# A gated mix of memory attention and a ReGLU layer: later places for the gate's row products, and a new written-out order of work

## The chip, the cores and the metric

The kernel runs on one core of one Trainium2 chip. The metric is device time in microseconds (us), the median of several runs; less is better. Before the change it was 268.71 us, the median of three runs of 266.35, 268.71 and 269.01 us.

## What is computed

`x` is 2048 rows of 512 numbers in bfloat16. The result is `g * a + (1 - g) * b` with a gate for each row, `g = sigmoid((x * gate_w).sum(-1))`.

```
a (attention with memory): q, k, v = x @ wq, x @ wk, x @ wv, 32 heads of 16; 4 segments s of 512 rows
    a_dot = softmax(q_s k_s^T / 4 + causal mask) v_s
    a_mem = phi(q_s) M / (phi(q_s) z);   phi(t) = t + 1 if t > 0, else exp(t)
    o = sigmoid(beta) * a_mem + (1 - sigmoid(beta)) * a_dot
    M, z = M + phi(k_s)^T v_s, z + sum phi(k_s)       (used by the next segment)
    a = o @ wo
b (ReGLU layer): b = (relu(x @ W_gate) * (x @ W_up)) @ W_down,   512 -> 1792 -> 512
```

The sum inside the gate, `(x * gate_w).sum(-1)`, is what is called the gate's row product here: one VectorE instruction for 128 rows.

## The kernel before, in words

**Work and stages.** The four segments are pipelined. `proj(s)` (L528) makes q, k and v of a segment, `att(s)` (L633) its attention, `mu(s)` (L581) the memory products phi(k)^T v that are added to `M`, `nd(s)` (L602) the part read from the memory, `ffn(s)` (L729) the 14 column blocks of `W_gate` and `W_up`, and `outp(s)` (L753) the four output tiles with `wo` and `W_down`. While the attention of one segment runs, the projections of the next, the ffn of this one and the outputs of the last one are put between its pieces on TensorE.

**PSUM.** There are eight banks. Four (`psL`) hold the logits of one attention quad; the next quad has to wait until ScalarE has made the exponentials of the last (`exp`, L651). The other four (`psA`) are handed out in turn to everything else: one bank for each accumulation, as one *epoch*. A bank may be written anew when all readers of the epoch before it are done. The list `BANKS` says which bank each new epoch gets. So a matmul can be held up by a VectorE or ScalarE instruction that has still to empty a bank.

**The names used below.** `wg0_8` and `wu0_8` are the products of column block 8 of `W_gate` and `W_up` for segment 0 (L739), two halves of two matmuls each. `relu0_8` (L747 on ScalarE, L748 on VectorE) empties the bank of the first into `rl`; `hm0_8` (L750, VectorE) multiplies the bank of the second with it into `hT` and so frees that bank. `q2_1`, `k2_1` and `v1_2` are projections (L544, L546), emptied by `qcp2_1`, `kcp2_1`, `vcp1_2` (VectorE at L555, L559, L572, ScalarE at L551). `quad0_2C` is one attention quad (L647), `pv0_1` a product of exponentials and values (L679), emptied by two transposes `tr0_1_0`, `tr0_1_1` (L689); after it come `rden`, `rdg`, `ad` and `bt` (L696 to L705) on VectorE. `kmask` (L563, L564) makes the masked k, and `kts`, `kphi`, `qts`, `qphi` (L525, L526) the phi of k and q.

**The gate (L481 to L513).** The rows of segment 0 are in `hT` already. For the twelve row tiles 4 to 15 the SP queue loads 128 rows into one shared buffer, `osb` slot 2 (`ldxr4` to `ldxr15`, L494), and VectorE makes the product `gate4` to `gate15` (L497) from it, in place. With one buffer, `ldxr5` waits for `gate4`. The four sums of a segment go through `gexp` and `omg1` on ScalarE, and by way of a scratch tensor in DRAM (`gwr`, `grd`, L504 and L506) they are spread for `rdg`.

**What sets the order.** Nothing is scheduled on the chip. Every operation is put into a queue of one engine (L390 to L513, L820 to L851). `ORDER` (L24) is a text with a letter for each operation: the letter names the queue, and the next operation of that queue that is not done is placed. Operations that two engines can do (`relu`, `qcp`, `kcp`, `vcp`, `kmask`, `fin`) stand in queues of both, so the letter also picks the engine. `place` (L204) puts the operation at the end of its engine's program, with the semaphore waits that it needs. Every engine then does its program strictly in this order. The times in the code (a cost for each operation, `LAT`, and `op.after`, the earliest time of an operation) are what the order was planned with; in `place`, `after` is read for DMAs alone (L230), and the costs decide nothing there but which of 16 DMA semaphores a transfer gets (L232). The order itself stands in the text.

**The loads of the gate** have planned earliest times (L495): `GATE_T` is 44000 ns for tiles 4 to 7, 90000 for 8 to 11 and 140000 for 12 to 15, and 4000 ns more for each further tile.

Of the kernel before, what the change touches and what calls it, by code (L numbers as in the profile page):

```python
# [21 lines left out]

LETTERS = "abcdefghijklmnopqrstuvwxyzABCDEFGHIJKLMNOPQRSTUVWXYZ0123456789"
ORDER = (  # L24
    "gefafafefafefafefaefaggfgagggggahgihaisggsagggsgsahgsigssahsisssasbsssassssassssCassssBsasssCsasBabsasEsasHaEHsasyIaDpasaIwsIasDasaFsaysSIapsaFSwauIau"
    "FasLubSsIapjFSuwSukaunuLSuKSapkuwnuVuLSuSVnuKpdunwuLSudSuLSuSmRpdmuKkSswLSudlnuSLuSsokKRsCuSRUpswRuUDSssSLsUCSsIpJDSqUSwQsIozSsuCIpzSsxSszdSswDSssQdsB"
    "uESudIpJLsSSwsdRsFSuuLsxScpzqFSwuPszqcLToTyzpSsTzwuScuFSsTLsSszySpcSsFSwuBSsszcRuuELSUpSuzwunUuzsuLSKouSIpJuLSwuSzsSsLSssBSEsSQpCuQwsuRsRqDUySpSLuSwUz"
    "uSuzunuKuzSopLKSuSwIuuzIuzssKLSpSCszSuwSnuuLsSouEQqLSySpzVswsVzsFsuzGSpnuwuzLSsSuzuKszSpmSGouSwrLtSSOtOuOmStnpWStSwItIortSOtOtOSuSNpWSLtwSsXstFSqSpztw"
    "szsztBtSpztwzortSOztStSMSpOXStwOStStIWtIrntxtOSoOtSOxpSuSMWswtQXuRsRqESpnUtwuPSuLUTuTLuTtAopqLSTQuwzSuStzSuLuSpzsSLwSuntuzoQsKpBSuwStzuuILSuJSuLSptSzw"
    "sSnstDSsNSpAswXRuBSuSuLumSuLmoSpnqSLwSRuszUsSzuSEuUQKuzSpzsLSowuIuIuzsKSzuSuCLSuSrAKuuOOuLpuwOuuLqLSpSzVuwsVzuzuLuSpzsLwSuSDsSuzuKsSzsSGAsuSWGpSLswrsO"  # L30
    "tOFtSOpStwIWrItSOtOSotOtSWpStwStSMrXtOuxOSuOSpKtnWwtQuouQqLxSpSztSwuSzuQttLSptSnwtIotItzSNuzzpXuwSzuSuLStSLtSpnqwsAosPStTFtSqSTSpSzuwTtzSuTMuuzXStnKpz"
    "mtSzmowtuLSuSuzuSLuSKpSnuAwotIrLSttOItOSpOSuwSuSuLtuMSpuSLwXurLuuOuOSLpSuwSOuSuLuuLSqKSSpSzuwuzuLuuzKSpzuwzuuLSSuLuSpSzqSwLuAVzuVuSKzpSuwSzuzLSuuzuKpS"
    "zuSwLuSuSAuuLWSuLSpKuSWwSutLtuSpSuwSuLStttStSupLtwrtOtOMtSOXtSuSWtSrtOpOtOwuWtLttMSSqXSSpztwtztztzuzutSzuSuAtSKtSuNptXwutuLSpuSLwuLutqLSSpSzuwSuzuLuuz"
    "SuLSuKzpzuwuSzuSuAtKSuLSpuSLwSuuLuuSuStKSpLtSwutqSpSztwuzuMuuLKXSpuSzwSuzuLSvzvKpSzuwSuAuLSvSuSuKSuSvLuSuqKvzvzuvzuzvzvLvvzvvAvvvNvXNvvXvvvvvvNvvvXvvv"
    "vvvvNvvvvvXMX"
)
BANKS = (
    "012312301230123012301231021302130120123102132031201320321031203102130123012302300123121202312102102101201031203123012010231023120302030201201203203203"
    "10202012010231023102310213021302023001321310230230230320302021032132132130"
)  # L40


# [275 lines left out]
def program(sc, nc, T, PL, PA, A_x, A_wq, A_wk, A_wv, A_wo, A_beta, W_g, W_u, W_d, gate_w, out, NSEG, KT, NF, NT, EPS, SCALE):  # L318
    V = type("V", (), T)

    def op(eng, fn, occ, **k):
        return sc.add(Op([(eng, fn, occ)], **k))

    def pe(fn, occ, **k):
        k.setdefault("lat", PE_LAT)
        if k.get("role") == "w":
            k["reads"] = list(k.get("reads", ())) + [f"init{i}" for i in range(4)]
        return op("pe", fn, occ, **k)

    def dve(fn, occ, **k):  # L330
        return op("dve", fn, occ, **k)
# [151 lines left out]
    gq = {"pe": [], "act": [], "dve": [], "pool": [], "sp": []}  # L483
    for c in range(NSEG):
        t0, t1 = 4 * c, 4 * c + 4
        gx = V.gexp[:, t0:t1]
        if c == 0:
            for t in range(4):
                gq["dve"].append(dve(lambda e, t=t: e.tensor_tensor_reduce(out=V.hT[:, t, :], in0=V.hT[:, t, :], in1=V.gwb[:], scale=1.0, scalar=0.0, op0=ALU.mult, op1=ALU.add, accum_out=V.gl[:, t:t + 1]),
                                     690, reads=[f"hT{t}", "gwb"], writes=[f"hT{t}", f"gl{t}"], name=f"gate{t}"))  # L490
                gq["dve"][-1].after = 5800.0
        else:
            for t in range(t0, t1):
                ld = dma("sp", lambda e, t=t: e.dma_start(V.osb[:, 2, :], A_x[0, t * 128:(t + 1) * 128, :]), 1 << 17, writes=["osb2_0", "osb2_1"], name=f"ldxr{t}")  # L494
                ld.after = GATE_T[c] + 4000.0 * (t - t0)  # L495
                gq["sp"].append(ld)
                gq["dve"].append(dve(lambda e, t=t: e.tensor_tensor_reduce(out=V.osb[:, 2, :], in0=V.osb[:, 2, :], in1=V.gwb[:], scale=1.0, scalar=0.0, op0=ALU.mult, op1=ALU.add, accum_out=V.gl[:, t:t + 1]),  # L497
                                     690, reads=["osb2_0", "osb2_1", "gwb"], writes=["osb2_0", "osb2_1", f"gl{t}"], name=f"gate{t}"))
# [79 lines left out]
    def va(s):  # L578
        return [f"va{s % 2}_{tt}" for tt in range(4)] + ["vone"]

    def mu(s):  # L581

        ep = Epoch()

        def fn(e):
            for G in range(4):
                for tt in range(4):
                    for j in range(4):
                        ins = e.matmul(A(ep)[32 * j:32 * j + 32, 34 * G:34 * G + 34], lhsT=V.phik[:, tt, 128 * G + 32 * j:128 * G + 32 * j + 32],  # L589
                                       rhs=V.vaug[:, s % 2, tt, 8 * G + 2 * j:8 * G + 2 * j + 2, :].rearrange("q h c -> q (h c)"),  # L590
                                       start=(tt == 0), stop=(tt == 3), tile_position=(0, 32 * j), skip_group_check=True)
            return ins
        m = pe(fn, 300.0, reads=[f"phik{g}" for g in range(4)] + va(s), name=f"mu{s}", ep=ep, role="w", mode="c")
        d = dve(lambda e: e.tensor_tensor(V.Mc[:], V.Mc[:], A(ep)[:, 0:136].rearrange("q (g c) -> q g c", g=4), ALU.add), t_dve(136), reads=["Mc"], writes=["Mc"], name=f"mum{s}", ep=ep, role="r")
        ps = []
        for G in range(4):
            j3 = lambda t, G=G: t[:, G, :].rearrange("q (j c) -> q j c", c=34)
            ps.append(pool(lambda e, G=G, j3=j3: e.tensor_tensor(j3(V.Mbd16), V.Mc[:, G, :].unsqueeze(1).to_broadcast([128, 4, 34]), j3(V.mumask), ALU.mult), t_pool(136, 2.2),
                           reads=["Mc", "mumask"], writes=[f"Mbd16_{G}"], name=f"mu16_{s}"))
        return m, d, ps  # L600
# [32 lines left out]
    def att(s, between):  # L633
# [26 lines left out]
        def flush():  # L660
# [229 lines left out]
```

## Time and profile before

| | |
|---|---|
| median of 3 runs | 268.71 us (266.35 to 269.01) |
| the profiled execution | 265.84 us, of which its span is 264.1 us |
| granted TensorE clock, mean | 1.0 |
| instructions | 6633 |
| HBM read, written | 9.87 MB, 2.11 MB |
| DMA packets | 34684, 24032 of them under 512 B |

The span runs from the first to the last instruction of the program in the one execution that was profiled; all rows of the trace are of that execution. PE is TensorE, PEld its weight loads, DVE VectorE, ACT ScalarE, POOL GpSimd, and SPq the queue of SyncE that issues nearly all DMAs. In the timeline, a row is: start in us, length in us, engine, line, operation, output and inputs; in square brackets the time that the engine was idle before it and what ended that. The length of a matmul row includes its fill and drain, which overlap the next one, so the pace of TensorE is read from one start to the next.

### The profile page before, as it was taken

The numbers are of one execution on the slowest core, as the hardware profiler recorded it, in microseconds if no ns is written. First come the engines' busy times: TensorE is split into PE (matmuls) and PEld (weight loads), VectorE is DVE, ScalarE is ACT, GpSimd is POOL, SyncE is SP. The second block draws the span as 40 slices with busy tenths as digits, with TensorE's granted clock in tenths as the row PEclk, the third lists the DMA queues.
The fourth block names the chain that finished last, engine by engine and source line by source line (L and its number), as shares of the span: only waits on it lengthen the run. The fifth ranks groups of instructions, "written<-read, shape, count | busy, mean of one in ns | idle before, by whom it ended". The sixth has DMA issues, their size and how long they took to land.

```text
span 264.1 us, 6633 instructions
## 1 busy us (share of the span) xinstructions
PE 259.3 (98%) x2761; PEld 115.3 (44%) x2761; DVE 189.8 (72%) x367; ACT 185.6 (70%) x160; POOL 121.4 (46%) x283
## 2 busy tenths in 40 slices
PE   8999999979999999999999999999999999999996
PEld 5533344334344444444444444344444444343444
DVE  5589887878886698899886696977973556746600
ACT  4689899869897686796676975776886356778021
POOL 3038555753645365755254466634653433536100
PEclk9999999999999999999999999999999999999999
DMA  6889673692131223102032410100130200000011
GB/s 182 243 310 262 145 62 65 188 291 43 40 88 21 62 61 81 43 20 43 4 84 42 99 43 22 21 24 2 40 87 0 60 22 22 0 2 20 2 40 40
DMA packets 34684, 19.34 MB, mean 73 GB/s; under 512 B 24032, under 2 KB 34144, under 8 KB 34656
## 3 DMA queue, kind: packets, MB, share of 16 engines
q1 hardware_dynamic: 34560, 18.93, 29.5%
q8 instruction: 21, 0.34, 0.6%
q14 instruction: 7, 0.06, 0.1%
q10 hardware_dynamic: 96, 0.00, 0.0%
HBM read 9.87 MB, written 2.11 MB: 45 GB/s over the span
## 4 chain that ended last, share of the span: by engine, by line
PE 98%; DVE 1%; issue 0%; DVEq 0%
PE psA L739 38%; PE psA L778 19%; PE psA L546 10%; PE psL L647 9%; PE psA L679 7%; PE psA L544 5%; PE psA L771 5%; PE psA L537 1%; PE psA L609 1%; PE psL L437 1%; PE psA L589 1%; PE psL L446 1%; DVE adT L700 0%; DVE hT L750 0%; PE psA L459 0%; DVE osb L787 0%
## 5 line engine op out<-in xcount | busy, mean ns | idle before, releaser
L656 POOL TENSOR_SCALAR_AFFINE_SELECT E<-E 64x256 bf16<-64x256 bf16 (+1 forms) x256 | 113.5, 454 | 119.2 <-ACT E L651 110.8
L651 ACT ACTIVATE E<-psL 128x2048 bf16<-128x2048 f32 x72 | 135.1, 1876 | 40.4 <-PE psL L647 37.8
L739 PE MATMUL psA<-xT,wg 128*128 128x512 bf16 x224 | 60.4, 380 | 1.6 <-DVE hT L750 1.6
L739 PE MATMUL psA<-xT,wu 128*128 128x512 bf16 x224 | 61.9, 380 | 0.0
L778 PE MATMUL psA<-wd,hT 128*128 128x512 bf16 (+2 forms) x238 | 58.9, 367 | 0.0
L750 DVE TENSOR_TENSOR hT<-psA,rl 128x512 bf16<-128x512 f32 x56 | 38.2, 685 | 20.3 <-PE psA L739 11.9
L739 PEld LDWEIGHTS psA<-xT,wg 128*128 128x128 bf16 x224 | 20.4, 98 | 27.2 <-DVE hT L750 2.3
L739 PEld LDWEIGHTS psA<-xT,wu 128*128 128x128 bf16 x224 | 20.3, 98 | 25.6 <-issue 4.1
L778 PEld LDWEIGHTS psA<-wd,hT 128*128 128x128 bf16 x238 | 21.0, 98 | 23.5 <-issue 3.6
L689 DVE STREAM_TRANSPOSE Tn<-psA 128x512 f32<-128x512 f32 x32 | 21.2, 696 | 11.3 <-PE psA L679 11.3
L647 PE MATMUL psL<-qT,kp 32*128 32x192 bf16 (+7 forms) x512 | 28.6, 287 | 0.0
L747 ACT ACTIVATE rl<-psA 128x512 bf16<-128x512 f32 x30 | 17.9, 596 | 9.6 <-PE psA L739 9.5
L748 DVE TENSOR_SCALAR rl<-psA 128x512 bf16<-128x512 f32 x26 | 17.8, 686 | 5.5 <-PE psA L739 5.3
L647 PEld LDWEIGHTS psL<-qT,kp 32*128 32x128 bf16 x512 | 8.2, 92 | 26.1 <-issue 10.2
L679 PE MATMUL psA<-E,vaug 64*17 64x128 bf16 (+7 forms) x512 | 18.7, 283 | 0.0
L679 PE MATMUL psA<-E,vsh 64*17 64x128 bf16 (+7 forms) x512 | 18.3, 283 | 0.0
L546 PE MATMUL psA<-xT,wk 128*128 128x512 bf16 x64 | 17.0, 380 | 0.0
L544 PE MATMUL psA<-wv,xT 128*128 128x512 bf16 x64 | 16.8, 380 | 0.0
L771 PE MATMUL psA<-wo,oT 128*128 128x512 bf16 (+2 forms) x68 | 16.5, 367 | 0.0
L679 PEld LDWEIGHTS psA<-E,vaug 64*17 64x17 bf16 x512 | 11.6, 86 | 8.3 <-issue 2.8
L787 DVE TENSOR_SCALAR osb<-psA,omg 128x512 bf16<-128x512 f32 (+1 forms) x9 | 6.3, 702 | 12.1 <-PE psA L771 10.5
L788 ACT ACTIVATE osb<-psA,omg 128x512 bf16<-128x512 f32 (+1 forms) x8 | 5.4, 673 | 13.3 <-PE psA L771 12.3
(72 smaller groups left out, 235.7 us busy)
## 6 DMA issues: line engine op xcount, KB each, us to landing
vsh<-vaug SPq DMA_DIRECT2D x8, 272.0 KB, 3.7
out_dram<-osb SPq DMA_DIRECT2D x15, 128.0 KB, 1.7
wg<-in_B_W_gate_dram SPq DMA_DIRECT2D x8, 224.0 KB, 6.1
wu<-in_B_W_up_dram SPq DMA_DIRECT2D x8, 224.0 KB, 5.8
wd<-in_B_W_down_dram SPq DMA_DIRECT2D x3, 512.0 KB, 5.7
osb<-in_A_x_dram SPq DMA_DIRECT2D x12, 128.0 KB, 2.3
hT<-in_A_x_dram SPq DMA_DIRECT2D x4, 128.0 KB, 2.2
wq<-in_A_wq_dram SPq DMA_DIRECT2D x4, 128.0 KB, 2.4
```

Source lines behind the costliest of these rows:

```text
L544: ins = e.matmul(A(ep)[:, :], lhsT=V.xT[:, kt, tok + col * 128:tok + (col + 1) * 128], rhs=w[:, kt, :], start=(kt == 0), stop=(kt == KT - 1))
L546: ins = e.matmul(A(ep)[:, :], lhsT=w[:, kt, col * 128:(col + 1) * 128], rhs=V.xT[:, kt, tok:tok + 512], start=(kt == 0), stop=(kt == KT - 1))
L647: ins = q.matmul(PL[:, jj, o:o + 512 - 64 * c], lhsT=V.kp[r, kslot(s, G), c, :], rhs=V.qT[r, qslot(s, G), 64 * c:512], start=True, stop=Tr ...
L651: acts.append(act(lambda a: a.activation(V.E[:, e, :, :], PL[:, :, :], ACT.Exp, scale=SCALE), t_act(2048), reads=[f"bankL{b}" for b in ran ...
L656: pools.append(pool(lambda g, ap=ap, base=base: g.affine_select(out=ap, in_=ap, compare_op=ALU.is_ge, fill=0.0, base=base, pattern=[[0, 4] ...
L679: ins = q.matmul(A(eps[p])[32 * jj:32 * jj + 17, 64 * c:512], lhsT=v[:, 8 * G + 2 * jj + p, :], rhs=V.E[r, e, jj, o:o + 512 - 64 * c], sta ...
L689: ds.append(dve(lambda e, p=p, ep=eps[p]: e.transpose(V.Tn[:, p, :], A(ep)[:, :]), 706, writes=[f"Tn{p}"], name=f"tr{s}_{G}_{p}", ep=eps[p ...
L739: ins = e.matmul(A(ep)[:, :], lhsT=w[:, kt, f * 128:(f + 1) * 128], rhs=V.xT[:, kt, c * 512:(c + 1) * 512], start=(kt == 0), stop=(kt == K ...
L747: evs.append(sc.add(Op([("act", lambda e, ep=eg, r=r: e.activation(V.rl[:, r, :], A(ep)[:, :], ACT.Relu), t_act(512)), ("dve", lambda e, e ...
L750: evs.append(dve(lambda e, ep=eu, r=r, hs=hs: e.tensor_tensor(V.hT[:, hs, :], A(ep)[:, :], V.rl[:, r, :], ALU.mult), t_dve(512), reads=[f" ...
L771: ins = e.matmul(A(ep)[:, 0:c1 - c0], lhsT=V.oT[:, o0 + G, i * 128:(i + 1) * 128], rhs=V.wo[:, G, c0:c1], start=st_ and G == 0, stop=sp_ a ...
L778: ins = e.matmul(A(ep)[:, 0:c1 - c0], lhsT=V.hT[:, slots[f], i * 128:(i + 1) * 128], rhs=V.wd[:, f, c0:c1], start=st_ and f == f0, stop=sp ...
```

## The change

Three things are changed.

1. Each gate product of the tiles 4 to 15 gets a planned earliest time, 8000 ns after that of its load. For `gate4` that is 52000 ns.
2. The planned cost of a memory product `mu` goes from 300 to 420 ns.
3. `ORDER` and `BANKS` are new throughout, laid out with these two numbers.

The instructions themselves stay as they are.

```
-    "gefafafefafefafefaefaggfgagggggahgihaisggsagggsgsahgsigssahsisssasbsssassssassssCassss...
+    "gefafafefafefafefaefaggfgagggggahgihaisggsagggssaghgssigsahssissasbsssassssassssCassss...
...
                 gq["dve"].append(dve(lambda e, t=t: e.tensor_tensor_reduce(out=V.osb[:, 2, :], in0=V.osb[:, 2, :], in1=V.gwb[:], scale=1.0, scalar=0.0, op0=ALU.mult, op1=ALU.add, accum_out=V.gl[:, t:t + 1]),
                                      690, reads=["osb2_0", "osb2_1", "gwb"], writes=["osb2_0", "osb2_1", f"gl{t}"], name=f"gate{t}"))
+                gq["dve"][-1].after = ld.after + 8000.0
...
-        m = pe(fn, 300.0, reads=[f"phik{g}" for g in range(4)] + va(s), name=f"mu{s}", ep=ep, role="w", mode="c")
+        m = pe(fn, 420.0, reads=[f"phik{g}" for g in range(4)] + va(s), name=f"mu{s}", ep=ep, role="w", mode="c")
```

Read with the queues, both texts hold the same 1513 operations. Around `gate4` the VectorE programs are:

```
before: tr0_1_0 vcp1_2 hm0_7 tr0_1_1 vcp1_3 qcp2_0 rden0_1 kphi1_1 relu0_8 rdg0_1
        gate4 ad0_1 hm0_8 kmask1_3_0 hm0_9 bt0_1 relu0_10 qcp2_1
after:  tr0_1_0 tr0_1_1 vcp1_2 hm0_7 relu0_8 rden0_1 kts1_1 rdg0_1 qcp2_0 ad0_1 kphi1_1
        gate4 qcp2_1 kmask1_3_0 kmask1_3_1 bt0_1 hm0_8 hm0_9 qts1_3
```

and TensorE's programs, from the quad `quad0_2E` on (a product that stands twice is its two halves):

```
before: quad0_2E v1_2 wu0_7 wu0_7 v1_3 v1_3 q2_0 quad0_2C q2_0 wg0_8 k2_0 k2_0 wg0_8 wu0_8 quad0_2D
        wu0_8 wg0_9 wg0_9 q2_1 wu0_9 wu0_9 quad0_3A wg0_10
after:  quad0_2E wu0_7 v1_2 wu0_7 v1_3 wg0_8 wg0_8 v1_3 quad0_2C q2_0 q2_0 k2_0 k2_0 wu0_8 q2_1 quad0_2D
        q2_1 wu0_8 wg0_9 wg0_9 wu0_9 quad0_3A wu0_9 wg0_10 k2_1 k2_1 q2_2
```

The SP queue's first 75 issues, which end with `ldxr8`, are in the same order in both. Behind them, some loads of the gate, stores and transposes change places: `ldxr9` goes behind the last transpose of `amem` and a store, `ldxr10` and `ldxr11` behind two transposes of `ek`, `ldxr14` behind a store.

Of the operations with a choice of engine, on balance two `relu`, one `kcp` and three `kmask` go from VectorE to ScalarE, and four `qcp` the other way.

More of the change, by code (lines that the diff above doesn't have):

```diff
@@ L24 @@
 ORDER = (
[L25 to L32, printed above, removed]
@@ L33 @@
-    "zuSwLuSuSAuuLWSuLSpKuSWwSutLtuSpSuwSuLStttStSupLtwrtOtOMtSOXtSuSWtSrtOpOtOwuWtLttMSSqXSSpztwtztztzuzutSzuSuAtSKtSuNptXwutuLSpuSLwuLutqLSSpSzuwSuzuLuuz"
-    "SuLSuKzpzuwuSzuSuAtKSuLSpuSLwSuuLuuSuStKSpLtSwutqSpSztwuzuMuuLKXSpuSzwSuzuLSvzvKpSzuwSuAuLSvSuSuKSuSvLuSuqKvzvzuvzuzvzvLvvzvvAvvvNvXNvvXvvvvvvNvvvXvvv"
+    "gefafafefafefafefaefaggfgagggggahgihaisggsagggssaghgssigsahssissasbsssassssassssCassssBsasssCsasBabsasEsasHaEHsasyIaDpasaIwsIasDasaFsaysSIapsaFSwauIau"
+    "FasLubSsIapjFSuwSukaunuLSuKSapnuwukuLSVuSLuVSuSndpKuwnuduLSuSuLSduKSkpRmuwkdsLSuSRsosBKSUsSsmREsnUSpJIsBlwusRuDUssxSLpSqUBSwSIsozsuzJSpSsDwSsdzSuIsBds"
@@ new lines @@
+    "KSpIsEQdswSQuuduFSsSLysScpzqFSwsPuzqcLToySzpTuSzwsSczuTsSFuTxuSLcsSLpSGsSzwsRszcBsuzsEpRswnUuuBSuSUIuKpIuzSwouSLsSsSLsSEQuuQKpsSRwuBSuuSLqKSRypuzSUSwu"
+    "zuSUsLuzuSKnpuwsIoLSuSsDSuJSszpLSCuSwzsusQuLSuESnpKqzwSoszVsVzuGuSzuSyLpSszSwzsusFszuKSuSFpStnwLtSrtOumOSmopOStwSnWtItIuSrLtSpSOtOwSotOSMtqSWSpzswtXzs"
+    "ztFrtSOpztOSwzttoOStSzWNSrtSOxpOSXtOStwIWtIsQttRxpSRswtBStSMsSuQXpntwAosQuuDSuStLSKqSRpUqPSRuUwzStTuzTUuTLuSpzKuTUnwtuzoSuzuuLKSpuSzwSuLStSuIuLJSpSsnw"
+    "stAosBSsSuQEpSLtwSuSMuuXLuSqnLmSpmouSwzuSuzunsLSpuzSwLSuSsIosBuKSszuJzsEuLSSszuSCrApKuOOwuOuuLuLuSpSLqwuzVuVzuSKsSzpSzuwzsuSDuuLKSpzuSwSsAsLSWssFSpGrS"
@@ new lines @@
+    "ItwOSIttOStOStopSrWSwtSOtOtOtMWStSprXwuOtOtuOtxSLpWSqSwQtzSutzxSuSnpswsLSosSFtuzNSuIpJXLSuSwuzuQuLSuLsSpzGqwtnPSotzTqTQpzSuwTtzStSAttnptzSwouzzttSMTuz"
+    "XStSKpAuwLSuStntuLSmpJSoIuwuSLtStSuStmSLrStOSunoNOpOuwuLuuXLruSOuOSKpOSuwSuLuqLSpSzuwSuzSuLuuzKSpzuwzuuLSSuzuSKpSAqwLSuzVuVzuSKpSzuwSzuLSuuzuKpSzuSwLu"
+    "SuSAuuLWSuLSuKSuWSpLuwutLtStSrpSOtOwSuOtWtuSpLtSwttMtXSpuSwStSttqSSpSztwStzuztLtNSztzXtrSzuStOSOptOwtWuqLSpSzuwuztLuuzSpztwztMSSuAXuuzSKpStAwtSLtSuSuL"
+    "SuSuKSuSpLuwuuLutLSuSuSuKSpuwuLtuqLSSpzuwuzuLuuzKSuzuzuuLSKSpzuSwuAtLuuLSuSvLSpuSwtuMuuLXSuSuLSvKSuvvuvLquzuzvKvzvzuzvuzvLvvAvvvvNvXNvvXvvvvvvNvvvXvvv"
@@ L37 @@
 BANKS = (
-    "012312301230123012301231021302130120123102132031201320321031203102130123012302300123121202312102102101201031203123012010231023120302030201201203203203"
-    "10202012010231023102310213021302023001321310230230230320302021032132132130"
+    "012312301230123012301320132013201320312032012031023123013201320130231023102301313120101312302302302320323201320132012012301230132030203013013023021010"
+    "21313012012301230123012301230131230302012012320320320320320320321321321310"
 )
```

## The prediction, as put on record

> **What bounds the kernel now.** I read the page's first lines, then the chain that ended last, then the waits of TensorE alone, and then the one stretch in which it waits.
>
> ```profile
> PE 259.3 (98%) x2761; PEld 115.3 (44%) x2761; DVE 189.8 (72%) x367; ACT 185.6 (70%) x160; POOL 121.4 (46%) x283
> ...
> PEclk9999999999999999999999999999999999999999
> ...
> PE 98%; DVE 1%; issue 0%; DVEq 0%
> ...
> L739 PE MATMUL psA<-xT,wu 128*128 128x512 bf16 x224 | 61.9, 380 | 0.0
> ```
> ```profile
> PE psA L739 <- DVE hT L750: 1.6, 1, 1.6
> PE psL L437 <- PEq L875: 0.8, 1, 0.8
> ```
>
> TensorE is the bound: busy 259.3 of 264.1 us, at full clock, and it waits only twice, at its start and once for VectorE's `hT` (L750). A busy engine isn't proof of full pace, so I look at starts:
>
> ```profile
> 112.94 1.03 PE L739 MATMUL psA<-xT,wg 128*128 128x512 bf16 x4
> 113.81 0.59 PE L739 MATMUL psA<-xT,wu 128*128 128x512 bf16 x2
> 114.33 0.40 PE L647 MATMUL psL<-qT,kp 32*128 32x512 bf16 x4
> 114.66 0.60 PE L778 MATMUL psA<-wd,hT 128*128 128x512 bf16 x2
> ```
>
> Four matmuls take 0.87 us from start to start, 0.216 each; the row's 380 ns is mostly overlap. A quad costs 0.09 going in (0.52 less two matmuls of 0.216) and holds TensorE for 0.33. So the time is a fixed sum of matmuls, changes of kind, and waits. An order can gain only what it takes from the last two. The one wait, in the timelines of VectorE, SP and TensorE:
>
> ```profile
> 49.77 0.69 DVE L555 CAST qT<-psA 128x512 bf16<-128x512 f32 x1 [0.27 <-PE psA L546]
> 50.38 0.34 DVE L696 RECIPROCAL rden<-Tn 128x32 f32<-128x32 f32 x1
> 50.64 0.63 DVE L526 TENSOR_TENSOR ek<-ek,ttmp 128x1024 bf16<-128x1024 bf16 x1
> 52.11 0.40 DVE L698 TENSOR_TENSOR rdg<-rden,gexpT 128x32 f32<-128x32 f32 x1
> 54.64 0.69 DVE L497 CUSTOM_DVE_ANT_0 osb<-osb,gwb 128x512 bf16<-128x512 bf16 x1 [2.14 <-DMA osb<-in_A_x_dram]
> 55.26 0.88 DVE L700 TENSOR_TENSOR adT<-Tn,rdg 128x512 bf16<-128x512 f32 x1
> 56.07 0.68 DVE L750 TENSOR_TENSOR hT<-psA,rl 128x512 bf16<-128x512 f32 x1
> 56.67 0.38 DVE L563 TENSOR_SCALAR kp<-kT,pm 128x512 bf16<-128x512 bf16 x1
> 56.97 0.67 DVE L750 TENSOR_TENSOR hT<-psA,rl 128x512 bf16<-128x512 f32 x1
> ```
> ```profile
> 42.06 5.95 SPq L383 DMA_TRANSPOSE xT<-in_A_x_dram  x4
> 48.06 0.58 SPq L354 DMA_DIRECT2D wo<-in_A_wo_dram  x1
> 48.69 0.51 SPq L354 DMA_DIRECT2D wd<-in_B_W_down_dram  x1
> 49.24 1.10 SPq L494 DMA_DIRECT2D osb<-in_A_x_dram  x1
> ```
>
> VectorE stands 2.14 us before `gate4`, whose load was issued at 49.24 and landed at 54.6, 5.4 us later. Behind it wait `ad0_1` and `hm0_8` (the L750 row of 56.07); `hm0_8` has to empty the bank that `wg0_10` takes, so TensorE goes on at 56.80.
>
> ```profile
> 45.77 0.40 PE L647 MATMUL psL<-qT,kp 32*128 32x256 bf16 x8
> 46.10 0.60 PE L544 MATMUL psA<-wv,xT 128*128 128x512 bf16 x2
> 54.85 0.40 PE L647 MATMUL psL<-qT,kp 32*128 32x512 bf16 x4
> 56.80 1.04 PE L739 MATMUL psA<-xT,wg 128*128 128x512 bf16 x4 [1.56 <-DVE hT L750]
> ```
>
> From 54.85 a quad holds TensorE to 55.18, so the hole is 1.62 us by starts. It is all that the new order could take back by ending waits.
>
> **The change part by part.** *The instructions.* Both orders hold the same operations, and counted over the text, TensorE changes its kind of matmul 164 times in either. The sum of its work is the same: 0. So is the end: the last outputs from `oa3_0` on stand in the same order.
>
> *The memory product's cost* is a number of the plan; here a real one is:
>
> ```profile
> 160.09 0.59 PE psA L589 x64
> ```
>
> It changes no instruction: 0. The plan with 300 ns had no hole behind a memory product that the waits of TensorE show, so I give nothing for the better number.
>
> *The moves between engines.* On balance two `relu` (596 ns on ScalarE, 686 on VectorE), one `kcp` (597, 691) and three `kmask` (714, 402) go to ScalarE, and four `qcp` (597, 688) come back:
>
> ```profile
> L747 ACT ACTIVATE rl<-psA 128x512 bf16<-128x512 f32 x30 | 17.9, 596 | 9.6 <-PE psA L739 9.5
> L748 DVE TENSOR_SCALAR rl<-psA 128x512 bf16<-128x512 f32 x26 | 17.8, 686 | 5.5 <-PE psA L739 5.3
> L551 ACT ACTIVATE kT<-psA 128x512 bf16<-128x512 f32 x8 | 4.8, 597 | 4.6 <-PE psA L546 4.6
> L555 DVE CAST qT<-psA 128x512 bf16<-128x512 f32 x8 | 5.5, 688 | 2.6 <-PE psA L537 2.0 <-PE psA L546 0.6
> L564 ACT ACTIVATE kp<-kT,pm 128x512 bf16<-128x512 bf16 x4 | 2.9, 714 | 0.0
> L563 DVE TENSOR_SCALAR kp<-kT,pm 128x512 bf16<-128x512 bf16 x28 | 10.7, 402 | 2.2 <-PE psL L647 1.2 <-ACT kT L551 1.0
> ```
>
> ScalarE: 2 x 596 + 597 + 3 x 714 - 4 x 597 = +1.5 us; VectorE: 4 x 688 - 2 x 686 - 691 - 3 x 402 = -0.5 us. The cover is their idle 30% and 28%: 0. Without it, at most the 1.5 us would show.
>
> *The gate's product* is the part that counts. Its planned time in the new text is 52000 ns. The load lands at 54640 in this execution, and the SP queue issues the same 75 DMAs first, so nothing makes it land sooner. Nor does `gate4` come late enough to miss that: I now walk both engines through the new order. TensorE stands at 45.77 in both at `quad0_2E`. From there to `wg0_10` are 19 half products of 0.432, four quads of 0.33 and three entries of 0.09: 8.21 + 1.32 + 0.27 = 9.80, due at 55.57. VectorE's last instructions before `gate4` are `qcp2_0`, `ad0_1` and `kphi1_1`. `q2_0` is issued by 45.77 + 9 x 0.432 + 2 x 0.33 + 0.09 = 50.41 and drained 0.16 later (a row of two lasts 0.59 or 0.60, not 0.43); then come 0.61 (49.77 to 50.38), 0.81 (55.26 to 56.07) and 0.63: free at about 52.6, as before (52.11 + 0.40 = 52.51), and idle for 2.0 us. `gate4` runs at 54.64 again and the next starts at 55.26. What stands behind it is now `qcp2_1`, two `kmask`, `bt0_1`, then `hm0_8`:
>
> ```profile
> 45.66 0.70 DVE L703 STREAM_TRANSPOSE oT<-adT 128x512 bf16<-128x512 bf16 x1
> 46.29 0.67 DVE L689 STREAM_TRANSPOSE Tn<-psA 128x512 f32<-128x512 f32 x1
> ```
>
> `qcp2_1` frees the bank of `wg0_10` at 55.26 + 0.69 = 55.95; with the 0.06 seen before (56.07 + 0.68 to 56.80, rounded) TensorE goes on at 56.01, a hole of 0.44. `q2_2` comes 1.30 later (three half products), at 57.31, and takes the bank of `hm0_8`. That starts at 55.26 + 0.61 + 2 x 0.30 + 0.63 = 57.10 and ends at 57.78; TensorE goes on at 57.84, a second hole of 0.53. `wu0_10` needs `hm0_9` at 58.7, which ends at 58.4. Sum of the holes 0.97 instead of 1.62: **-0.65 us**. The ends: a load landed by 52.6 leaves no hole, -1.62; one 1 us later than in this execution makes holes of 1.97, +0.35 against it (the old order would then have 2.62). I take -0.65, since the SP rows that decide the landing come ahead of anything that moves.
>
> *What `gate4` shifts behind it.* `ldxr5` waits for `gate4` to free the buffer; SP is issuing two transposes until then, `kT21_0` about 0.8 us later than before as `kphi1_1` is done later. Its readers in the next segment have tens of us. 0.
>
> *The other gates.* Their loads wait for nobody near TensorE's path, and no wait of VectorE on them shows but the one:
>
> ```profile
> L497 DVE CUSTOM_DVE_ANT_0 osb<-osb,gwb 128x512 bf16<-128x512 bf16 x12 | 8.5, 706 | 2.1 <-DMA osb<-in_A_x_dram 2.1
> ```
>
> So more distance there is worth 0. Where SP's issues change places (`ldxr9` behind two, `ldxr10` and `ldxr11` behind two transposes, `ldxr14` behind a store), I count TensorE's work between load and product in the new text: 7.3, 4.7, 5.0 and 4.1 us, and 4.3 for `ldxr15`. Against the usual landing that is ample:
>
> ```profile
> osb<-in_A_x_dram SPq DMA_DIRECT2D x12, 128.0 KB, 2.3
> ```
>
> *The sum.* Span 264.1 - 0.65 = 263.45 us; with the 1.74 around it, 265.19 for an execution like the profiled one, 265.84. That one lies 2.87 under the median of the runs and 2.18 under their mean of 268.02. Three runs in two clumps make a poor median, so I go from the mean: **267.4 us**. What holds the runs up isn't in the trace; a late load at `gate4` would hold up both orders alike.
>
> [...]
>
> **The rivals.** *The wait at `gate4` ends altogether.* It would need `ldxr4` to land by 52.6. The usual 2.3 us would do it; against it speak the unchanged issues ahead of it. Holes 0: -1.62, 264.2 against the profiled execution, 266.4 against the mean.
>
> *Slower: later gate loads land like the first one, in 5.4 us.* Place: `gate10`, `gate11`, `gate14`, `gate15`, whose distances are 4.7, 5.0, 4.1, 4.3 us. VectorE would wait 0.7 + 0.4 + 1.3 + 1.1 = 3.5 us, and with nothing spare TensorE as long: 267.4 + 3.5 = 270.9, over 1% more than 268.0. It begins with a landing of 4.1 us and decides only near 5.4. For it speaks that transposes now go ahead of `ldxr10`; against it, that distances of 5.0, 4.7 and 4.2 us at `gate10`, `gate11` and `gate14` stood without a wait in the profile of before.
>
> *Slower by the clock.* At the start five matmuls take 2.29 us, twice the pace of later:
>
> ```profile
> 0.84 2.29 PE psL L437 x5
> ```
>
> If the load lands 2.5 us later still, the hole is 3.5 us; were the clock halved after it for as long as at the start (some 5 us), that costs 2.5 + 2.5: 272.4. Against it: the hole of 1.6 us left the clock at full. [...]
>
> **How the numbers follow.** Mine 0.70, the wait gone 0.16, late loads 0.10, the clock 0.04. A measurement of this kernel can't tell less than about 1% from no change. Mine and the first rival are faster by over 1% of 268.7 (under 266.0) only if the runs fall like the profiled one, 265.2 or 264.2: 0.08 of each: faster 0.16. Slower is the two last, 0.14; the same 0.70. The range reaches from halfway between those two lows, 264.8, to 270.2, short of the late loads; within it my own case lies between 265.2 and 268.4, the profiled execution and the slowest run less 0.65.
>
> **What would show it.** Right: VectorE idles some 2 us before the first L497 row, at about 54.6; TensorE has two holes near 56 and 57.5 of about 0.4 and 0.5 us, on L555 and L750; none later; 164 changes of kind and the end in step. Wrong: no DMA wait at L497 (first rival); waits at later L497 rows; a hole on a bank that I took for free; a span more than 1 us off 263.45.

## The result, and the profile after

| | before | after |
|---|---|---|
| median of 20 runs each (the three of the section on the time before are among them) | 267.40 us (265.21 to 270.95) | 265.02 us (264.70 to 266.98) |
| ratio, after to before | | 0.9933, 95% interval 0.9905 to 0.9960 |
| profiled execution | 265.84 us, span 264.1 | 265.18 us, span 263.2 |

The ratios, here and below, leave out runs over 1.5% above the fastest of their kernel, which all have a mean granted clock of 0.994 or less where it was recorded, while the medians leave out none; what these runs are comes out in the experiments.

So the new order is 0.4 to 1.0% faster, and within 1%. The profiled execution came to 265.18 us, where my sum for such an execution was 265.19. That they meet to 0.01 is luck: the span is 263.2 us where I had 263.45, and the time around it came to 1.9 us where I had 1.74. The page's engine line, its chain, and the waits of TensorE alone:

```profile
PE 259.5 (99%) x2761; PEld 115.2 (44%) x2761; DVE 189.3 (72%) x365; ACT 186.4 (71%) x162; POOL 124.7 (47%) x283
...
PE 90%; SPq 4%; DVE 2%; DMA 2%; issue 0%; DVEq 0%
```
```profile
PE psL L437 <- PEq L876: 0.8, 1, 0.8
PE psA L547 <- DVE hT L751: 0.4, 1, 0.4
```

TensorE is the bound as before. Its longest wait for VectorE has shrunk from 1.6 to 0.4 us, and stands at another matmul: at L547, which is `q2_2`. The chain tells the rest. Before, it ran through TensorE for 98%; now it leaves TensorE at that matmul and goes back by way of VectorE, the load of gate4's rows and the SP queue. In this part of the chain, in order of time (start, length, what):

```profile
47.86 0.58 SPq L354
48.45 0.04 issue
48.49 0.51 SPq L354
48.99 0.04 issue
49.04 5.36 DMA osb<-in_A_x_dram
54.40 0.02 issue
54.42 0.69 DVE osb L497
```

The load is in flight for 5.36 us and lands at 54.40. The timelines of VectorE and TensorE around it (`...` stands for rows left out):

```profile
54.42 0.69 DVE L497 CUSTOM_DVE_ANT_0 osb<-osb,gwb 128x512 bf16<-128x512 bf16 x1 [1.56 <-DMA osb<-in_A_x_dram]
55.04 0.69 DVE L556 CAST qT<-psA 128x512 bf16<-128x512 f32 x1
...
56.97 1.24 DVE L751 TENSOR_TENSOR hT<-psA,rl 128x512 bf16<-128x512 f32 x2
```
```profile
45.90 0.40 PE L648 MATMUL psL<-qT,kp 32*128 32x256 bf16 x8
...
55.31 0.61 PE L740 MATMUL psA<-xT,wu 128*128 128x512 bf16 x2
55.78 0.60 PE L740 MATMUL psA<-xT,wg 128*128 128x512 bf16 x2
56.22 1.03 PE L547 MATMUL psA<-xT,wk 128*128 128x512 bf16 x4
57.67 0.60 PE L547 MATMUL psA<-xT,wq 128*128 128x512 bf16 x2 [0.42 <-DVE hT L751]
...
59.07 0.40 PE L648 MATMUL psL<-qT,kp 32*128 32x448 bf16 x8
```

VectorE still stands, 1.56 us, before `gate4`. `qcp2_1` (the L556 row) now comes directly behind it, so `wg0_10` starts at 55.78, only 0.04 later than the 0.43 us of the two matmuls from 55.31 ask for. At `q2_2` the next start is 57.67, while the four matmuls from 56.22 take until 57.09 at the usual pace: a hole of 0.58. Together 0.62.

**A measure for all that follows.** The same TensorE work lies between `quad0_2E` (the 32x256 row) and `quad0_3B` (the 32x448 row). I call the time from the one start to the other the *stage*: 59.07 - 45.90 = 13.17 us here. Before, `quad0_3B` starts at 59.93:

```profile
59.93 0.40 PE L647 MATMUL psL<-qT,kp 32*128 32x448 bf16 x8
```

So the stage was 14.15 us (unrounded; 45.77 is in the prediction). Runs without any wait in it (below) show 12.53. So the stage held 1.62 us of holes before and 0.64 after. From `quad0_3B` to the first weight load of the last output tile it is 199.76 us in both: nothing else moved. The start, up to `quad0_2E`, took 45.77 and 45.90; it differs from run to run.

### The profile page after: what moved, and what is told of

Read it like the earlier page. It is cut to its first block, busy times and chain, and to the rows that moved or that the text cites. A ratio compares the mean times of both kernels' runs of the same rounds, so it can differ in the third digit from the quotient of the medians.

```text
span 263.2 us, 6640 instructions
## 1 busy us (share of the span) xinstructions
PE 259.5 (99%) x2761; PEld 115.2 (44%) x2761; DVE 189.3 (72%) x365; ACT 186.4 (71%) x162; POOL 124.7 (47%) x283
## 4 chain that ended last, share of the span: by engine, by line
PE 90%; SPq 4%; DVE 2%; DMA 2%; issue 0%; DVEq 0%
PE psA L740 35%; PE psA L779 19%; PE psL L648 8%; PE psA L547 7%; PE psA L680 6%; PE psA L772 5%; PE psA L545 4%; SPq L383 2%; DMA osb<-in_A_x_dram 2%; PE psA L538 2%; PE psA L610 1%; PE psL L437 1%; SPq L507 1%; SPq L570 1%; PE psL L446 1%; DVE Tn L690 0%
## 5 line engine op out<-in xcount | busy, mean ns | idle before, releaser
L657 POOL TENSOR_SCALAR_AFFINE_SELECT E<-E 64x256 bf16<-64x256 bf16 (+1 forms) x256 | 116.0, 464 | 114.6 <-ACT E L652 105.9
L748 ACT ACTIVATE rl<-psA 128x512 bf16<-128x512 f32 x32 | 19.1, 596 | 14.5 <-PE psA L740 14.5
L749 DVE TENSOR_SCALAR rl<-psA 128x512 bf16<-128x512 f32 x24 | 16.5, 688 | 6.8 <-PE psA L740 6.6
L547 PE MATMUL psA<-xT,wk 128*128 128x512 bf16 x64 | 17.1, 380 | 0.0
```

The costliest lines, as they stand in the source:

```text
L547: ins = e.matmul(A(ep)[:, :], lhsT=w[:, kt, col * 128:(col + 1) * 128], rhs=V.xT[:, kt, tok:tok + 512], start=(kt == 0), stop=(kt == KT - 1))
L657: pools.append(pool(lambda g, ap=ap, base=base: g.affine_select(out=ap, in_=ap, compare_op=ALU.is_ge, fill=0.0, base=base, pattern=[[0, 4] ...
L748: evs.append(sc.add(Op([("act", lambda e, ep=eg, r=r: e.activation(V.rl[:, r, :], A(ep)[:, :], ACT.Relu), t_act(512)), ("dve", lambda e, e ...
```

## The experiments

**Theories.** *Gate*: the whole gain is the time that TensorE loses to a late load at `gate4`; all else in the new text is worth nothing. *Rivals*: the better memory product number, the moves between engines, or other loads have a part; or the load's place in time, and not `gate4`'s place, is what counts. All profiles at one view, worked out from the rows' starts:

| | order | load lands | its landing after the start of the stage | holes in the stage | median, us | ratio to the order before, interval |
|---|---|---|---|---|---|---|
| before | old | 54.62 | 8.85 | 1.62 | | |
| after | new | 54.40 | 8.50 | 0.64 | 265.02 | 0.9933 (0.9905 to 0.9960) |
| e1 numbers only | old | 56.73 | 10.61 | 4.88 | 265.99 | 0.9989 (0.9957 to 1.0021) |
| e2 gate4 later | old | 55.40 | 9.10 | 0 | 264.54 | 0.9931 (0.9909 to 0.9953) |
| e3 gate4 later | new | 54.35 | 7.84 | 0 | 264.70 | 0.9945 (0.9924 to 0.9966) |
| e4 load first | new | 49.79 | 4.04 | 0 | 264.26 | 0.9927 (0.9899 to 0.9955) |
| e5 load first | old | 51.55 | 5.82 | 0 | 264.51 | 0.9956 (0.9930 to 0.9982) |
| e6 load one later | old | 55.93 | 10.04 | 3.99 | 269.15 | 1.0129 (1.0094 to 1.0163) |
| e7 load one later | new | 54.74 | 9.05 | 1.23 | 266.93 | 1.0047 (1.0018 to 1.0077) |
| e8 load three later | new | 57.72 | 11.73 | 5.81 | 269.90 | 1.0146 (1.0088 to 1.0204) |
| e9 quad later | old | 55.49 | 8.69 | 1.47 | 266.57 | 1.0001 (0.9969 to 1.0033) |
| e10 quad earlier | new | 53.61 | 6.62 | 0.33 | 265.78 | 0.9945 (0.9914 to 0.9976) |
| e11 gate4 early | new | 55.06 | 9.00 | 4.40 | 267.54 | 1.0034 (1.0001 to 1.0067) |
| e12 engines early | old | 55.03 | 9.18 | 1.96 | 266.52 | 1.0007 (0.9974 to 1.0039) |

The medians of the order before beside these runs were 266.71 (e1 to e4), 266.26 (e5 to e8), 266.45 (e9 to e11) and 265.85 us (e12). The rest of the program, from `quad0_3B` to the last output tile, took 199.76 or 199.77 us in all but e8 (199.92).

**e1. The two planned numbers alone.** The order stays as before.

```
+                gq["dve"][-1].after = ld.after + 8000.0
-        m = pe(fn, 300.0, ... name=f"mu{s}", ...)
+        m = pe(fn, 420.0, ... name=f"mu{s}", ...)
```

> The old order of work with the two new planned numbers alone. Theory: the numbers act only through the order, so this is the old kernel: 1.000 of its time within 0.5%, a hole of TensorE of 1.3 to 2 us near 56 us, span near 264. Rival, that the numbers themselves change waits: a span under 263.5 and no hole.

0.9989 (0.9957 to 1.0021): the numbers by themselves do nothing that can be measured. But the execution that was profiled took 269.71 us, and shows what holds such runs up. The load was issued at 51.02 and landed at 56.73, so TensorE stood still twice as long as before, and then went at half pace:

```profile
55.20 0.40 PE L648 MATMUL psL<-qT,kp 32*128 32x512 bf16 x4
58.72 1.48 PE L740 MATMUL psA<-xT,wg 128*128 128x512 bf16 x4 [3.13 <-DVE hT L751]
59.99 1.06 PE L547 MATMUL psA<-xT,wq 128*128 128x512 bf16 x2
60.85 1.89 PE L547 MATMUL psA<-xT,wk 128*128 128x512 bf16 x4
```

Four matmuls take 1.89 us in place of 1.03. The stage is 4.88 us longer than without a hole: 3.19 of standing still (from 55.20 and the 0.33 of its quad to 58.72), 1.69 of half pace.

**e2 and e3. `gate4` later still, in either order.** VectorE's program:

```
e2, order before:   rdg0_1  -gate4  ad0_1  hm0_8  kmask1_3_0  hm0_9  +gate4  bt0_1
e3, new order:      kphi1_1 -gate4  qcp2_1 kmask1_3_0 kmask1_3_1 bt0_1 hm0_8 hm0_9  +gate4  qts1_3
```

> The old order with one product moved: gate4 goes behind hm0_9, three instructions of VectorE later, all else in place. Theory: the hole near 56 us is all that this wait costs, and only through hm0_8 queued behind it: no wait of VectorE on L497, no hole, span 264.1 - 1.6 = 262.5, about 0.994 of the old time or a little less; if this wait also makes the old kernel's runs differ (265.2 to 271.0), they close up to some 2 us. Rival, that the new order gains by something else (other loads, the moved copies): a hole goes but the time stays within 0.2% of the old, or the runs stay as far apart.

> The new order with gate4 behind hm0_9, six instructions of VectorE later. Theory: the wait of 1.56 us on L497 goes, with it the hole of 0.4 us before q2_2: span 263.2 - 0.6 = 262.6, 0.6 us faster than the new order, 0.991 of the old or less. Rival, that something else now holds TensorE at that place (the bank of q2_2 by another reader): the span stays at 263.2.

Both stages are 12.53 us, without a wait at L497. The span of e3 is 263.2 us all the same and not 262.6, and its ratio is 0.9945 where I had 0.991 or less: the stage began at 46.51, 0.61 us later than in the new order, and the start differs from run to run. One move in the old order gives all that the new order gives: 264.54 us, 0.9931 where that has 0.9933. And its twelve runs lie between 263.92 and 265.47, where the 31 of before lay between 264.18 and 271.17. So the spread of the runs came from this one load as well.

**e4 and e5. The load first, in either order.** SP's program, the same edit in both:

```
 ldx3_3
+ldxr4
 ldwo
 ldwd0
-ldxr4
 ldwd4
```

> The new order with the load of gate4 moved on the SP queue ahead of wo and the first part of wd, two issues. Theory: it lands late because 768 KB are issued just ahead of it: issued near 47.9, it lands by 52, VectorE waits less than 0.3 us, no hole, span 262.6. Rival, that the DMA engines are behind by the transposes anyway: it still takes 5 us, lands at 53, VectorE waits 0.3 to 0.8 us (a hole of up to 0.1), and wo and wd land later by as much.

> The order before with one move: the load of gate4's rows is issued on SP right behind the third x chunk, ahead of the loads of W_o and W_down, as the run of the new order with the same move had it (there it was issued at 46.51 and landed at 49.79). Theory (the whole gain is gate4's wait for its load): VectorE doesn't wait at L497, TensorE has no hole, the span is about 262.5 and the ratio about 0.993, the same within 0.2% as the new order with the same move (264.26), although every other piece stands where the order before has it. Rival (the other 164 moved pieces, mu's number and the engine moves are worth something of their own): the order before stays slower than the new order with the same move by more than 0.3%, at 265.2 or above.

Ahead of the two loads of 512 KB (1024 KB, not the 768 of the expectation) the flight is 3.3 us (e4, 46.51 to 49.79) and 4.1 (e5, 47.44 to 51.55), and nobody waits. The stage of e5 by its two quad rows is 12.53, like e4's:

```profile
45.73 0.40 PE L647 MATMUL psL<-qT,kp 32*128 32x256 bf16 x8
...
58.26 0.40 PE L647 MATMUL psL<-qT,kp 32*128 32x448 bf16 x8
```

With the load out of the way the two orders are equal: 264.51 and 264.26 us, 0.1% apart, with the same stage and the same rest. (They ran on different chips; the ratios to the order before, 0.9956 and 0.9927, have intervals that overlap.) The other changed places, the memory product's number and the moves between engines are worth nothing that can be measured.

**e6, e7, e8. The load later.** SP's program: `ldxr4` behind `ldwd4` in the order before (e6) and in the new one (e7), and behind `ldwd12` in the new one (e8).

```
e6, e7:  ldwd0 -ldxr4 ldwd4 +ldxr4 ldwd8 ldwd12
e8:      ldwd0 -ldxr4 ldwd4 ldwd8 ldwd12 +ldxr4
```

> The order before with gate4's load issued one transfer later on SP (behind ldwd4). From the spacing of the issues (0.55 us each) and the landing of the profiled run of before (54.6) the load should land near 55.5 to 56.5, and the first hole, 1.62 at 54.6, grows one for one to 2.5 to 3.5. Theory of the clock (a hole of about 3.2 us halves TensorE's clock for some microseconds, which added 1.69 us in the profiled run of the order before with the two numbers): around half of the runs or more show a granted clock of about 0.994 and spans of 266.3 and above, and the median is 267 to 269, ratio 1.002 to 1.01. Rival (only the landing counts, the clock plays no part and the lower granted clock comes from elsewhere): the runs stay at a clock of 1.0, with the median up by no more than the later landing, 0.9 to 1.9 us, and spans spread evenly.

> The new order with the same delay of gate4's load (behind ldwd4). Landing as there, 55.5 to 56.5. The new order's first hole opens only when the landing passes about 54.4, so it is 1.1 to 2.1, and 0.58 at the memory product stays: holes of 1.7 to 2.7, span 263.7 to 265.0, ratio 0.993 to 1.0. Theory: no single hole reaches 3 us, the granted clock stays at 1.0 in nearly all runs, and the run is 2 us or more ahead of the order before with the same delay. Rival (what I had predicted, that a late load holds up both orders alike): the new order is only about 0.65 to 1.0 ahead of the order before with the same delay, and shows the lower clock as often.

> The new order with gate4's load issued two transfers later still (behind ldwd12). Landing about 57.5 to 58.5, first hole 3.2 to 4.1. Theory of the clock: the hole passes 3.2 us, the rows behind it show matmuls at about half pace for some 4 us, the granted clock of the run is about 0.993, and the span is 262.5 + 3.7 + 0.6 + 1.7 = about 268.5, time about 270.4. Rival (no clock effect): the clock is 1.0 and the span about 266.8, time about 268.7.

All six runs of e6 have a mean clock of 0.993 or 0.994, and its median is 2.9 us above before, more than I had written (1.0129 against at most 1.01). Eleven of twelve of e7 stay at 0.999 or 1.0, and it is 2.2 us ahead of e6; it too is slower than I had written (1.0047 against at most 1.0). The profiled execution of e7, with the load at 54.74, is the fastest of its twelve (265.57), so it doesn't show what the others waited for. In e8 the four runs have 1.0, 0.994, 0.987 and 0.987. The hole in e6, and the granted clock (last column but two) in half microseconds:

```profile
54.97 0.39 PE L647 MATMUL psL<-qT,kp 32*128 32x512 bf16 x4
57.92 1.89 PE L739 MATMUL psA<-xT,wg 128*128 128x512 bf16 x4 [2.55 <-DVE hT L750]
```
```profile
57.00:57.50 0.50, 0.00 (x0) 0.00 (x0) 0.50 (x2) 0.30 (x1) 0.14 (x1) 0.81 1.75 203
57.50:58.00 0.50, 0.08 (x1) 0.09 (x2) 0.50 (x2) 0.00 (x0) 0.43 (x2) 0.50 0.74 114
...
60.50:61.00 0.50, 0.50 (x3) 0.20 (x2) 0.34 (x2) 0.00 (x0) 0.00 (x0) 0.77 0.00 0
```

A mean of 0.81 over half a microsecond is 0.31 at full and 0.19 at half clock, so the clock fell at 57.31; 0.77 is 0.23 at half, so it came back at 60.73; the rows between the two show 0.50. It was halved for 3.42 us. Where TensorE works all that time, that costs 1.7 us, as in e1 (1.69); in e6 the first 0.61 us of it lie in the hole, and it costs 1.4. Over a span of 264 us this is a mean clock of 0.9935, which is the 0.994 of all such runs; 6.83 us of half clock over the 268.7 of e8 are the 0.987 that it shows. So the lower clock of some runs isn't an outside disturbance. It is the second half of the price of a hole: of the 100 runs of the order before beside these experiments 19 have it (0.990 to 0.994), all with spans of 266.1 us and more, and every run above 265.8 is one of them. In the 20 runs of the new order there is none, and in the 44 of e2 to e5, without the hole, none is under 0.996.

**At the same landing.** The order before has holes of 1.62, 1.47 and 1.96 us where the load lands 8.85, 8.69 and 9.18 after the start of the stage (before, e9, e12): each time the landing less 7.22 or 7.23. The new order has 0.64 and 1.23 at 8.50 and 9.05 (after, e7): the landing less 7.86 and 7.82. So what the new order puts around `gate4` is worth 0.61 us at an equal landing.

**e9, e10, e12. Why does the load land earlier?** In the pair of profiles it landed 0.35 us earlier in its stage, and the runs ask for something like it. The mean span of the 100 runs of the order before is 264.8 us, that of the 81 without a halved clock 264.3, and that of the 20 runs of the new order 263.3. So, as an estimate over different chips, the gain is 1.5 us: 0.5 for the halved clock, 0.6 for what stands around `gate4`, and 0.4 left for an earlier landing. Up to e8 one thing went with it: in all profiles of the order before the small write `gscr<-gexp` took 4.4 to 5.3 us, in all of the new one 1.6, and SP came to the first of the loads behind it at 47.4 to 48.7 us and at 46.2 to 47.9. These are the rows of the transfers from 32 to 39 us, before and then after (size, median us to landing; the first row is a packet of an instruction queue, which the new order has between 29 and 30 us instead):

```profile
q14 instruction: 1, 0.01, 0.4%
...
gscr<-gexp SPq DMA_DIRECT2D x1, 2.0 KB, 5.1
```
```profile
gscr<-gexp SPq DMA_DIRECT2D x1, 2.0 KB, 1.6
```

e9 and e10 exchange TensorE's pieces there (e10 lets the two keep their banks); e12 puts seven pieces of 22 to 34 us on the engine of the new order:

```
e9, order before:   k1_1 +q1_2 +q1_2 quad0_1C pv0_0 -q1_2 -q1_2 wg0_6
e10, new order:     wu0_5 -q1_2 -q1_2 quad0_1C pv0_0 +q1_2 +q1_2 k1_2
e12, order before:  relu0_2, qcp1_0, qcp1_1, kmask1_0_1 to VectorE; relu0_3, kcp1_0, kmask1_0_0 to ScalarE
```

> The order before with one exchange on TensorE some 20 us ahead of gate4: q1_2's two pieces go ahead of quad0_1C and pv0_0 instead of behind them, as the new order has it, so that those two start some 0.9 us later (32.9 to about 33.8). No piece of gate4 or of its load is touched. What it asks: in the five profiles of the order before so far, the 2 KB write gscr<-gexp took 4.4 to 5.3 us to land and SP came to the load of W_o at 47.4 to 48.7; in the five of the new order the write took 1.6 us and SP came there at 46.2 to 47.9. Theory (TensorE's code load, a packet of the instruction queue, which comes at quad0_1C, overtakes the write in the order before, and SP's queue is held up behind it): the write lands in about 2 us or less, SP comes to W_o's load 0.5 to 1.3 us earlier, at 46.3 to 47.3, gate4's load lands at 53.0 to 54.1, the hole is 0.2 to 1.2, and the median is 264.8 to 265.6, ratio 0.993 to 0.996, though gate4 stands where it stood. Rival (the delay comes from elsewhere: the other instruction packet, or the engine moves): the write stays at 4.4 to 5.3 us, and the time stays within 0.2% of before.

> The new order with the opposite exchange: quad0_1C and pv0_0 go ahead of q1_2's two pieces on TensorE, some 0.9 us earlier (34.0 to about 33.1). Theory: the code load now meets the write gscr<-gexp or the transposes right behind it, the write takes 4 us or more, SP comes to W_o's load at 47.4 or later, gate4's load lands at 54.4 to 55.5, holes of 0.6 to 1.7, median 265.2 to 266.3. Rival: the write stays at 1.6 us and the time stays at the new order's, 264.8 to 265.1; a wait of TensorE at pv0_0 for its masks, of some 0.1 to 0.5, may come on top in both.

> The order before, with the seven pieces between 22 and 34 us (relu0_2, relu0_3, qcp1_0, kcp1_0, qcp1_1 and two kmask1_0) on the engine, ScalarE or VectorE, that the new order gives them; nothing else changes place, and TensorE, SP and gate4 stand as before. The exchange on TensorE left the write gscr<-gexp at 5.2 us, with the packet of instruction queue q14 at 33 us as in all profiles of the order before; in all of the new order that packet comes at 28 to 29 us and the write takes 1.6. Theory now (the two engines' instruction streams set when the packet comes): it moves to 28 to 30 us, the write lands in about 1.6, SP comes to W_o's load 0.5 to 1.5 us earlier than 48.0, gate4's load lands at 53.2 to 54.2, and the median falls by 0.4 to 1.3 us against before, ratio 0.995 to 0.9985. Rival (it is the place of some other piece, or a stream that these moves don't touch): the packet stays at 32 to 34, the write at 4.4 to 5.3, and the time within 0.2% of before.

My theory of TensorE's code load fell: in e9 the write still took 5.2 us, in e10 still 1.6. The median of e10, 265.78, lies where that theory had put it (265.2 to 266.3), but by luck, as it lost its time elsewhere: TensorE waited 1.0 us in all for exponentials of ScalarE, its stage began at 46.98 us, 1.08 later than in the new order, and VectorE didn't wait for the load at all, which landed at 53.61. The 0.33 us of hole in its stage lie between two starts at 48.19 and 48.73, ahead of `gate4`. In e12 the instruction packet stayed at 32 us, yet the write landed in 1.6, and SP came to the loads 1.1 us sooner than before:

```profile
46.95 0.58 SPq L354 DMA_DIRECT2D wo<-in_A_wo_dram  x1
47.58 0.51 SPq L354 DMA_DIRECT2D wd<-in_B_W_down_dram  x1
48.12 0.50 SPq L494 DMA_DIRECT2D osb<-in_A_x_dram  x1
```

It didn't help: this load was in flight for 6.9 us and landed at 55.03, and the time stayed (1.0007). So here an earlier issue alone did not land the load earlier, with the loads of 512 KB still ahead of it. In the nine profiles with the load at the place among SP's issues that both orders have, it landed at 54.62, 56.73, 55.40, 55.49, 55.03 in the order before and at 54.40, 54.35, 53.61, 55.06 in the new one. What makes that 1 us between the medians, and whether it would last over more profiles, stays open.

**e11. `gate4` three places earlier in the new order.**

```
 rdg0_1
+gate4
 qcp2_0
 ad0_1
 kphi1_1
-gate4
 qcp2_1
```

> The new order with gate4 three places earlier on VectorE, right behind rdg0_1 and so ahead of qcp2_0, ad0_1 and the phi_k product. Theory (only how much TensorE work lies between a late gate4 and the first bank that VectorE frees behind it counts): with the load landing at 54.4 qcp2_0 ends at about 55.8, wg0_9 waits for its bank from 53.6 on, a hole of about 2.2 in place of 0.64, span about 264.8, time about 266.7, ratio about 1.0; with a load later by 0.5 the hole passes 2.6 and the clock of such runs falls to 0.994. Rival (place doesn't count, only that the load is earlier in the new order): the time stays at 265.0.

267.54 us, 1.0034 (1.0001 to 1.0067) of the order before: three places on VectorE undo all that the new order had gained. `wg0_9` waits for the bank that `qcp2_0` empties behind `gate4`:

```profile
55.08 0.80 DVE L497 CUSTOM_DVE_ANT_0 osb<-osb,gwb 128x512 bf16<-128x512 bf16 x1 [4.48 <-DMA osb<-in_A_x_dram]
55.81 0.68 DVE L556 CAST qT<-psA 128x512 bf16<-128x512 f32 x1
```
```profile
53.31 0.59 PE L740 MATMUL psA<-xT,wu 128*128 128x512 bf16 x2
56.55 1.04 PE L740 MATMUL psA<-xT,wg 128*128 128x512 bf16 x4 [2.64 <-DVE qT L556]
```

By starts the hole is 2.81 us (from 53.31 and the 0.43 of two matmuls to 56.55), then comes a halved clock: 4.40 us in all. At this landing, 9.00, the new order would have 1.16 (9.00 less 7.84), so the hole itself is 1.65 us longer, where I had expected 1.56 (2.2 for 0.64). So the place does count, and the rival that only the load's time matters is out.

## Why the prediction was right, and where it was not

- *TensorE is the bound, and its instructions sum up alike*: right. The rest behind the stage is 199.76 us in both.
- *The number of the memory product and the moves between engines, 0*: right; e1 0.9989, e12 1.0007, and e5 against e4.
- *`gate4` goes on waiting*: right, 1.56 us where I had 2.0. The rival that the wait goes altogether is out for this order; e4 made it come true with a move of the load.
- *Two holes, 0.44 at `qcp2_1`'s bank and 0.53 at `hm0_8`'s, sum -0.65*: the two places are right, and they measured 0.04 and 0.58, as the load landed earlier and the stage began later. At an equal landing the new order saves 0.61.
- *The load lands at 54.64 again, since the issues ahead of it don't change*: wrong in size. It was 0.22 us earlier in the profiled execution (0.35 counted from the stage's start), and 1 us in the medians of nine profiles. The same list of issues didn't give the same landing. This is one place where the gain was more than my 0.65 us: the ratio stands for 0.4 to 1.0%, or 1.1 to 2.5 us.
- *"A late load at `gate4` would hold up both orders alike", and what holds the runs up isn't in the trace*: wrong. Us for us both pay alike, but the order before starts 0.61 us nearer to the hole that halves the clock (2.55 us did in e6), and 19 of its 100 runs paid for that. It was in the trace only of an execution that it had happened to; e1 brought one.
- *The clock after a hole of about 3.5 us, half of it for some 5*: my supposition, as nothing had shown it then: the hole of before, 1.56, left the clock at 1.0. The runs showed such a fall, to 0.50, with both sizes off: a hole of 2.55 was enough in e6, and it is 3.4 us of half clock at a price of 1.7 (e1) and 1.4 (e6), and twice as long in e8. (The five matmuls at the start, 2.29 us, go at half the later pace, not at twice, and the granted clock reads 1.00 there, so they show no halved clock.)
- *Later gate loads in 5.4 us*: no. L497 waits for a DMA once, at `gate4`, in all twelve products.
- *267.4 us from the mean of three runs*: 2.4 us too high. The base is 0.6 of that: 268.02 where the median of 20 runs is 267.40, and 265.85 to 266.71 in the 100 runs later. Two of the three, at 268.71 and 269.01, lie where the runs with a halved clock lie (their spans begin at 266.1, some 267.9 us), though their clocks weren't shown. The rest is the gain: the medians of 20 lie 2.4 us apart and not 0.65. What the sum put at nothing is the earlier landing and the halved clock, an estimated 0.4 and 0.5 us over all runs. From the profiled execution the sum gave 265.19 and the median came to 265.02, but that execution was one of the faster of the order before (four of the 20 runs are below its 265.84), so that this base came out so near is luck. The low end of the range, halfway between 265.2 and 264.2, would be 264.7 and not 264.8.

The quickest version is e4, 264.26 us: the load issued ahead of the bulk, in the new order. It isn't to be told from e2 and e3. It is 0.3% ahead of the new order as it stands (265.02, measured beside other runs).

## What to carry to other kernels

A small load that a product in the middle of the work waits for belongs ahead of bulk loads in its queue (3.3 and 4.1 us in flight there, 5.4 to 6.9 behind two of 512 KB); a planned time for the product doesn't move the load, and only buys as much as the work put in between. When runs of one order spread and one wait in the profile hangs on a DMA, let that load vary on purpose: what a wait costs isn't its length in one profile but what it costs at the landings that occur, with the halved clock (here 1.4 and 1.7 us for 3.4 of it) on top. And find out what makes a kernel's runs spread before a mean of three of them becomes the base of a forecast.

## What the runs showed of the hardware

The clock. In the profiled executions holes of up to 1.90 us of TensorE (e12; all by the rows' idle time) left the granted clock at 1.0; holes of 2.55, 2.64, 3.10 and 3.13 us (e6, e11, e8, e1) halved it. The fall comes with work or without: in e6 at 57.31, within the hole and 1.94 us after its start (54.97 and 0.40 make 55.37); in e1 behind the hole, since the four matmuls from 58.72 take 1.48 us, neither 1.03 nor 1.89. It then stayed down for 3.42 us in e6, for as long in e1 and e11, and for about twice that in e8. The first and the last row of it in e1, e11 and e8:

```profile
59.00:59.50 0.50, 0.50 (x3) 0.17 (x2) 0.50 (x2) 0.00 (x0) 0.00 (x0) 0.67 2.11 109
...
62.50:63.00 0.50, 0.50 (x3) 0.22 (x2) 0.47 (x2) 0.23 (x1) 0.00 (x0) 0.92 0.00 0
```
```profile
57.50:58.00 0.50, 0.45 (x2) 0.02 (x1) 0.50 (x2) 0.38 (x1) 0.00 (x0) 0.65 0.07 25
...
61.00:61.50 0.50, 0.50 (x4) 0.20 (x2) 0.47 (x2) 0.00 (x0) 0.43 (x2) 0.94 0.20 39
```
```profile
57.50:58.00 0.50, 0.00 (x0) 0.00 (x0) 0.26 (x1) 0.00 (x0) 0.43 (x2) 0.86 1.18 254
...
64.50:65.00 0.50, 0.50 (x9) 0.11 (x2) 0.00 (x0) 0.06 (x1) 0.00 (x0) 0.81 0.00 0
```

By the same reading that is from 59.17 to 62.58 (3.41 us), from 57.65 to 61.06 (3.41) and from 57.86 to 64.69, 6.83 us, twice as long. Behind the end of the program the clock falls once more, in e1 at 267.38, in before at 265.23 and in e12 at 264.93; these are the rows, each with TensorE's columns alone, and above the one of e12 its hole:

```profile
267.00:267.50 0.50, 0.00 (x0) 0.88 0.00 0
```
```profile
265.00:265.50 0.50, 0.00 (x0) 0.73 0.00 0
```
```profile
57.21 1.04 PE L739 MATMUL psA<-xT,wg 128*128 128x512 bf16 x4 [1.90 <-DVE hT L750]
...
264.50:265.00 0.50, 0.00 (x0) 0.93 0.00 0
```

How long TensorE has stood still doesn't decide it alone: in e6 and e8 1.94 and 1.85 us of the hole had passed when the clock fell (in e8 the last matmul ends at 56.01), while the whole 1.90 us of e12 left it at 1.0. Seven of the ten runs of e11 kept a clock of 1.0 at spans 1.9 to 3.1 us above that of e4, which had no hole; the holes of these seven weren't recorded. What else decides isn't shown by these runs. In e8 TensorE stood still for another 1.24 us behind the fall, and the clock was down for 6.83 us; in e6 for 0.61, and the clock was down for 3.42.

The flight of a load. The same 128 KB took 3.3 and 4.1 us ahead of the loads of 512 KB (e4, e5), and 5.4 to 6.9 behind two (nine profiles), 5.3 and 5.4 behind three (e6, e7) and 8.0 behind four and the last one of 256 KB (e8). The median of the twelve such loads of before is 2.3 us; the load at the head, 3.3 us, is still 1 us above it, and those behind the bulk are at more than twice.
